# Weight sums queued behind the last turn, later x loads, spread gates and reordered splits in an S4 + SwiGLU kernel

## The chip, the cores and the metric

One core of one Trainium2 chip runs the whole kernel. The metric is the device time in microseconds of one execution; the number compared is the median over several runs. TensorE is called PE in the profile, VectorE DVE, ScalarE ACT, GpSimd POOL, and SyncE SP; SP does nothing here but issue DMAs.

## The reference

The input is a sequence of L = 2048 rows of D = 640 values. It passes through two residual branches, each with a layer norm whose scale, shift and gate come from a small product `silu(c) @ w_mod`:

```python
x = A_u
h = _layernorm(x) * (1 + ca) + sa
x = x + ga * _A_ref(h, ...)          # S4: a long convolution per channel, over the whole sequence
h = _layernorm(x) * (1 + cb) + sb
x = x + gb * _B_ref(h, w1, w3, w2)   # SwiGLU

def _B_ref(x, w1, w3, w2):           # w1, w3: 640 x 1728, w2: 1728 x 640
    return (silu(x @ w1) * (x @ w3)) @ w2
```

Everything is float32. The change touches the second branch alone.

## The kernel before

**Stages.** The first 420 us or so compute the convolution. Then the second branch runs on four column blocks of 512 sequence rows, taken in two pairs; in each pair the two blocks are called A and B. The hidden width of 1728 is cut into 14 tiles of 128, f = 0 to 13; the last tile is half full and holds the halves of w1 and w3 beside each other.

**Products in float32.** TensorE multiplies a rounded type. Each operand is therefore split into a high part (a cast on ACT) and a low part (operand minus high part, on DVE), and a product takes three matmuls: high by high, high by low, low by high. The weights' parts are `gh`, `gl` (from w1, loaded as `wg`) and `uh`, `ul` (from w3, loaded as `wu`); both come from tiles `rw` of which there are five. A "turn" (`turn_a`, `turn_b`) transposes one of the five 128-row slices k of the normalized x on TensorE, evacuates it with scale and shift on ACT into a raw tile `s`, and splits it into a pair of tiles: `xA…`, `xB…`, and for k = 0 and 1 of the B block `T3…`, printed as `T`.

**Plain tiles and blocks.** Pair 0 takes four tiles f = 0, 13, 1, 2 in the plain way (`plain`): a gate product of 15 matmuls of 128x512 and, but for f = 13, an up product of 15; first the A pass in that order, then the B pass in the reverse order, 2, 1, 13, 0. Its first input slices are turned while the A pass runs: k = 4, 0, 2 between the two products of the last A tile, k = 3 and 1 after it. The other ten tiles, and thirteen in pair 1, go through `seven`: one tile for both column blocks at once, by a scheme with seven products instead of eight, 54 matmuls in all. It is called a block below, numbered n = 0 to 9 in pair 0. It needs differences of the x slices (`x_sums`, four instructions for each i = 0, 1, two on DVE and two on POOL, then split into T1, T2, T4) and four weight sums S0 to S3 of the next block (`w_sums` on POOL, from `rw` to `S`; `w_split` makes `S0h`, `S0l` and so on, on ACT and DVE). S1 reads S0, and S3 reads S1.

**Gates of the output weights.** `gate_w2(f)` loads a tile of w2 into `rw`, multiplies it on POOL by the gate row `gbr`, and stores it in the scratch tensor `w2s` with a DMA that POOL issues. All 14 are done during the ten blocks of pair 0, in the order f = 0 to 13: one in each block, two in blocks n = 3 to 6. `outputs` later loads them again (`rw<-w2s`), in the order of the tiles in `order`.

**What sets the order.** A scheduler orders most instructions of the second branch on each engine; each engine and the DMA queue of SP then run in that order, and an instruction that waits holds all behind it. `with tc.issue_after(ins)` puts the instructions traced in it behind `ins` on the engine of `ins`. All of this stage's instructions are recorded by one helper, so they have one line, L102, in the profile; they are told apart by their tiles.

**The change of pairs.** While the outputs of pair 0 run, `prepare` lays out by a table of steps (`at(n, fn)`) the turns of pair 1, its x sums and splits, the weight loads of its first plain tile (f = 13) and first block, and their splits. The four x tiles that it starts with (`x_next`, from the six `xm` tiles) are loaded in the code of block n = 6, with `issue_after` on the last matmul of the block before; that binds TensorE's queue only, and the loads stand on SP.

Of the kernel before, what the change touches and what calls it, by code (L numbers as in the profile page):

```python
# [2 lines left out]

# [27 lines left out]
NFT = 14  # L31
# [76 lines left out]
def tile_kernel(ctx: ExitStack, tc: tile.TileContext, a):  # L108
# [917 lines left out]
    def x_sums(i, parts=range(4)):  # L1026

        b11, b21, b12, b22 = xraw["A", i], xraw["A", i + 2], xraw["B", i], xraw["B", i + 2]
        for p in parts:
            out, l, r = ((b11, b12, b11), (b12, b22, b12), (b22, b22, b11), (b21, b21, b22))[p]  # L1030
            (G if p % 2 else V).tensor_tensor(out, l, r, op=OP.subtract)
        xraw["T1", i], xraw["T2", i], xraw["T4", i] = b11, b22, b21

    def x_sum_split(i, names=("T1", "T2", "T4")):
        for n in names:
# [17 lines left out]
    def weight(f, name):  # L1053
        if (f, name) in ahead:
            return ahead.pop((f, name))
        w = xp.tile([P, KD, P], F32, name="rw", bufs=5)
        w = w.rearrange("p k c -> p (k c)") if name in ("w2", "gated") else w
        if name == "gated":
            SQ.dma_start(w, w2s[f])
            return w  # L1060
        with tc.issue_after(zlast[0].ins):
            w_get(w, f, name, SQ)
        return w

    def gate_w2(f):

# [27 lines left out]
        g = split(weight(f, "wg"), WS, ("gh", "gl"), after)  # L1094
        return g, split(weight(f, "wu"), WS, ("uh", "ul"), after) if f < NFT - 1 else None

    def plain(c, f, h, ws, early=False, between=None):

        last = f == NFT - 1
        wgs, wus = ws  # L1100
# [3 lines left out]
        if early and f == 0:  # L1104
            pu = bank(1)
            for lo in range(2):
                for k in range(KD):
                    for ps, ws in ((pg, wgs), (pu, wus)):
                        for i in range(1 if lo else 2):
                            end = PE.matmul(ps, ws[i][:, k, :], x[k][lo], start=(k + i + lo == 0),  # L1110
                                            stop=(lo == 1 and k == KD - 1))
        else:
            end = prod3(pg, [(wk(wgs, k), x[k]) for k in ks], True, True)
            if between:
                with tc.issue_after(end.ins):
                    between()
            if not last:
                pu = bank(1)
                end = prod3(pu, [(wk(wus, k), x[k]) for k in ks], True, True)
        sg = room(8)  # L1120
        if not last:
            S.activation(sg, pg, AF.Silu)
# [172 lines left out]
    def prepare(q0, g):  # L1295
# [30 lines left out]
            at(n, lambda i=i: x_mid(4 * q0 + i, got[i], g))  # L1326
        for n, i, p in ((21, 0, 0), (22, 0, 1), (23, 0, 2), (24, 0, 3), (24, 1, 0), (24, 1, 1), (25, 1, 2), (26, 1, 3)):
            at(n, lambda i=i, p=p: x_sums(i, (p,)))
        for n, i, name in ((22, 0, "T1"), (24, 0, "T2"), (26, 1, "T1"), (26, 1, "T2")):
            at(n, lambda i=i, name=name: x_sum_split(i, (name,)))  # L1330
        at(24, lambda: fetch(NFT - 1, "wg"))
        at(26, lambda: first_block.append(blocks(0)))
        at(27, lambda: first_plain.append(plain_weights(NFT - 1)))
        at(27, lambda: w_sums(first_block[0], range(4)))
        at(28, lambda: w_split(first_block[0], (1, 0, 2, 3)))

# [12 lines left out]
    last_f = NFT - 1  # L1349
    output = iter(())  # L1350
    x_next, first_block, first_plain = [], [], []
    ungated = list(range(NFT))
    for pair in range(2):
        q0 = 2 * pair
        hA, hB = {}, {}
# [1 line left out]
        rest = [f for f in range(last_f) if f not in simple]  # L1357
        side = []
        ws = first_plain.pop() if first_plain else plain_weights(simple[0], last_sum)
        if pair == 0:  # L1360
            tiles = []
            x_first(tiles)
# [10 lines left out]
            sp_order[0] = False  # L1373
            mid = lambda i: (x_mid(4 + i, got[i], 0), x_norm(4 + i, got[i], tiles))
            turn = lambda *ks: [turn_b(1, tiles, k, 0) for k in ks]
            side = [lambda: (mid(0), mid(1)), lambda: (mid(2), mid(3)), None, lambda: turn(3, 1)]
        for n, f in enumerate(simple):
            hA[f] = h_tile()
            ws = ws or plain_weights(f, ends if pair == 0 and n == 1 else None)
            end = plain("A", f, hA[f], ws, pair == 0, (lambda: turn(4, 0, 2)) if n == 3 else None)  # L1380
            if n < len(simple) - 1:
                ws = None
            todo = side.pop(0) if side else None
            if todo:
                with tc.issue_after(end.ins):
                    todo()
            if pair == 0 and n == 1:
                with tc.issue_after(power[0].ins):
                    for j, (x, z, st) in enumerate(early):
                        G.dma_start(xs[j], x)  # L1390
        turned = ends[1]

        for n, f in enumerate(simple[::-1]):
            hB[f] = h_tile()
# [11 lines left out]
        next(output, None)  # L1406
        free = []
        order = rest[:10] + ([0, last_f, 1, 2] if pair == 0 else [last_f] + rest[10:])
        output = outputs(q0, order, (hA, hB), prepare(q0 + 2, 1) if pair == 0 else lambda n: None, pair == 1)
        if first_block:  # L1410
            W = block_split(first_block.pop())
        else:
            W = blocks(rest[0])
            with tc.issue_after(turned.ins):
                block_split(W)
                w_sums(W, range(4))
                w_split(W, (1, 0, 2, 3))
        for n, f in enumerate(rest):
# [6 lines left out]
            hB[f] = h_tile()  # L1425
            if pair == 0 and n == len(rest) - 4:
                x_next += [x_tile() for _ in range(4)]
                with tc.issue_after(end.ins):
                    for i in range(4):
                        SQ.dma_start(x_next[i], a["x"][(8 + i) * P:(9 + i) * P, :])  # L1430
            gates = [gate_w2(g) for g in ungated[:1 + (3 <= n < 7)]] if pair == 0 else []
            ungated = ungated[len(gates):]
            if nxt is None:
                next(output)
# [55 lines left out]
```

## Time and profile before

| what | value |
|---|---|
| median of 3 runs | 1000.11 us (998.22 to 1000.22) |
| the profiled execution | 1002.07 us, of which 1000.3 us is the span from its first to its last instruction |
| PE busy in the span | 921.3 us |
| DVE, ACT, POOL busy | 698.9, 540.1, 293.9 us |
| mean granted TensorE clock | 0.947 of full speed |

The span is that of one execution under the hardware profiler. Where a row gives a time for an engine, it is the start counted from the first instruction, then the duration; what stands in square brackets is how long the engine was idle just before and what released it. "SPq" is SP issuing DMAs; its durations are the time that the queue took for them, waits included. In a row of the stretches, the share of an engine that is not the bound is no loss.

### The profile page before, as it was taken

How to read it: one execution, taken by the hardware profiler on the slowest of the kernel's cores; microseconds unless marked ns; L12 is line 12 of the kernel's file. 1: busy time of each engine (PE TensorE's matmuls, PEld its weight loads, DVE VectorE, ACT ScalarE, POOL GpSimd, SP SyncE). 2: the span in 40 equal slices, each digit the busy share in tenths (PEclk: the TensorE clock that was granted, in tenths of full speed). 3: DMA queues.
4: the chain of work that ended last, by engine and by line, in shares of the span. 5: the costliest groups of instructions: out<-in, count | busy, mean ns of one | idle time of the engine just before them, and what ended most of it. 6: DMA issues, size and time to landing. Idle time of an engine off the chain costs nothing.

```text
span 1000.3 us, 20632 instructions
## 1 busy us (share of the span) xinstructions
PE 921.3 (92%) x8214; PEld 688.3 (69%) x8214; DVE 698.9 (70%) x1227; ACT 540.1 (54%) x793; POOL 293.9 (29%) x302
## 2 busy tenths in 40 slices
PE   5898797998988888797999999999999999999997
PEld 2545354666666666465888778777878888888886
DVE  4598856888898885665678666667796666664544
ACT  3668665999999973245433323355743333323432
POOL 1453333544444531114444450111142222200000
PEclk9855777999999999999999999999999999999999
DMA  9463586554566687695334432897441111113443
GB/s 268 154 230 116 201 197 188 147 154 120 146 161 160 163 217 224 207 240 207 113 111 132 145 132 63 214 280 218 133 145 53 53 53 53 52 41 86 151 147 116
DMA packets 106659, 149.91 MB, mean 150 GB/s; under 512 B 20964, under 2 KB 63076, under 8 KB 106564
## 3 DMA queue, kind: packets, MB, share of 16 engines
q1 hardware_dynamic: 101636, 133.93, 45.8%
q0 software_dynamic: 3424, 12.33, 3.6%
q10 hardware_dynamic: 1504, 2.36, 0.8%
q8 instruction: 64, 1.05, 0.4%
q14 instruction: 31, 0.25, 0.1%
HBM read 112.53 MB, written 36.04 MB: 149 GB/s over the span
## 4 chain that ended last, share of the span: by engine, by line
PE 43%; DMA 5%; POOL 3%; DVE 2%; issue 1%; ACT 0%; DVEq 0%; SPq 0%; POOLq 0%
PE ps L102 43%; DMA rw<-in_w_dram 2%; DMA w2s<-rw 2%; POOL S L102 1%; POOL rw L102 1%; DMA xs<-xm 1%; DMA rw<-in_wu_dram 1%; DVE xm L102 1%; POOL s L102 0%; DVE T L102 0%; DVE gl L102 0%; DVE s L102 0%; DVE ul L102 0%; DVE h L102 0%; DVE S2l L102 0%
## 5 line engine op out<-in xcount | busy, mean ns | idle before, releaser
L102 DVE TENSOR_TENSOR s<-ps,s 128x512 f32<-128x512 f32 x138 | 94.6, 686 | 68.9 <-PE ps L102 68.0
L473 POOL TENSOR_TENSOR ph<-thi,iota 128x1024 int32<-128x1024 int32 x40 | 85.4, 2134 | 175.9 <-DVE A L509 78.2
L102 DVE TENSOR_TENSOR gl<-rw,gh 128x640 fp32r<-128x640 f32 x87 | 77.6, 892 | 78.0 <-ACT gh L102 77.0
L102 ACT CAST gh<-rw 128x640 fp32r<-128x640 f32 x87 | 63.3, 727 | 109.9 <-PE ps L102 95.9
L571 PE MATMUL p<-uk,s 128*64 128x256 f32 x640 | 79.1, 389 | 13.6 <-PE pa L433 5.6
L102 PE MATMUL ps<-xA,gh 128*128 128x512 f32 x280 | 87.7, 392 | 0.6 <-ACT xA L102 0.4
L102 PE MATMUL ps<-gh,uh 128*128 128x512 f32 x224 | 87.5, 391 | 0.0
L102 PE MATMUL ps<-gl,uh 128*128 128x512 f32 x224 | 87.2, 389 | 0.0
L102 PE MATMUL ps<-gh,ul 128*128 128x512 f32 x208 | 81.1, 390 | 0.0
L571 PEld LDWEIGHTS p<-uk,s 128*64 128x64 f32 x640 | 45.2, 138 | 38.9 <-PE pa L433 8.4
L102 POOL TENSOR_TENSOR S<-rw 128x256 f32<-128x256 f32 x46 | 36.6, 798 | 116.2 <-DVE S0l L102 87.2
L102 PEld LDWEIGHTS ps<-xA,gh 128*128 128x128 f32 x280 | 52.3, 188 | 13.6 <-ACT xA L102 1.0
L102 PE MATMUL ps<-xA,gl 128*128 128x512 f32 x140 | 54.6, 390 | 1.1 <-DVE gl L102 1.1
L136 ACT ACTIVATE A<-pa 128x1024 f32<-128x1024 f32 x40 | 40.4, 1023 | 25.8 <-PE pa L433 24.4
L498 DVE TENSOR_TENSOR E<-A,cs 128x1024 f32<-128x1024 f32 x40 | 51.0, 1275 | 1.7 <-ACT A L136 1.7
L505 DVE TENSOR_TENSOR A<-A,ph 128x1024 f32<-128x1024 f32 x40 | 50.1, 1253 | 0.0
L613 PE MATMUL pz<-Y,i 64*128 64x128 f32 x640 | 45.4, 286 | 5.1 <-issue 3.1
L613 PEld LDWEIGHTS pz<-Y,i 64*128 64x128 f32 x640 | 39.2, 191 | 14.9 <-issue 11.4
L102 PEld LDWEIGHTS ps<-gl,uh 128*128 128x128 f32 x224 | 42.1, 188 | 9.0
L102 PEld LDWEIGHTS ps<-gh,uh 128*128 128x128 f32 x224 | 42.0, 188 | 8.8
L540 PE MATMUL pt<-s,K 128*64 128x128 f32 x640 | 47.3, 291 | 0.5 <-ACT uk L139 0.5
L522 PE MATMUL pk<-E 128*32 128x64 f32 x1280 | 46.6, 232 | 1.2 <-DVE E L501 0.6
(257 smaller groups left out, 2333.5 us busy)
## 6 DMA issues: line engine op xcount, KB each, us to landing
rw<-w2s SPq DMA_DIRECT2D x56, 320.0 KB
us<-u SPq DMA_DIRECT2D x16, 640.0 KB
s<-in_s_dram SPq DMA_DIRECT2D x40, 256.0 KB
i<-in_i_dram SPq DMA_DIRECT2D x40, 256.0 KB
rw<-in_wg_dram SPq DMA_DIRECT2D x31, 320.0 KB
rw<-in_wu_dram SPq DMA_DIRECT2D x28, 320.0 KB
uk<-us SPq DMA_DIRECT2D x32, 256.0 KB
zs<-zt SPq DMA_DIRECT2D x32, 256.0 KB
```

The costliest lines, as they stand in the source:

```text
L102: ins = fn(*args, **kw)
L136: return tc.keep_in_program_order(S.activation(*args, **kw))
L473: hold(G.tensor_tensor(p, bc(thi[:, sl], 2, NPH), bc(iota, 1, SD), op=OP.mult))
L498: keep(V.tensor_tensor(EC[s][:, :, 1:3, :], AA[s][:, :, 1:3, :], mid(cs[s]), op=OP.mult))
L505: keep(V.tensor_tensor(A[:, :, 1:3, :], A[:, :, 1:3, :], mid(ph[s]), op=OP.mult))
L522: keep(PE.matmul(pk[dq * 32:dq * 32 + 32, g, :], x[:, g * 4 + dq, 1, :], x[:, g * 4 + dq, 0:3:2, :], start=(st == 0), stop=(st == 1), tile ...
L540: keep(PE.matmul(pt[c * 64:c * 64 + 64, g, :], kk[:, g, :], s1[:, c, :], start=True, stop=True, tile_position=(0, c * 64)))
L571: keep(PE.matmul(p2[par * 64:par * 64 + 64, pi, c, :], s2[:, pi * 2 + par, c * 64:c * 64 + 64], uk[:, 0:kn + 1:kn, f, :], start=True, stop ...
L613: ins = keep(PE.matmul(pz[:, par, (g % 2) * 2 + pi, :], i1[r, pi, c, :], Y[r, pi, c, :], start=(c == 0), stop=(c == 1), tile_position=(par ...
```

## The change

Five edits, all in the second branch:

1. The turns of k = 3 and 1 of the B block are issued behind the ninth matmul of the up product of the last A tile (`then`), instead of behind its end.
2. The first block's splits, sums and sum splits in pair 0 are queued behind the last turn's instructions on ACT and DVE (`turned` is now both of them) and behind the last x sum on POOL (`summed`), instead of behind DVE's alone.
3. The x tiles of pair 1 are loaded behind the weight loads of block n = 6 on SP (`loaded`).
4. The output weights are gated in the order in which they are used, one per block, two in blocks 3 and 6, three in block 9.
5. At the change of pairs, the split of T2 of i = 1 goes behind the weight split of the plain tile, and the first block's weight splits behind that.

```diff
@@ x_sums
-            (G if p % 2 else V).tensor_tensor(out, l, r, op=OP.subtract)
+            summed[0] = (G if p % 2 else V).tensor_tensor(out, l, r, op=OP.subtract)
+    @contextmanager
+    def behind(*instrs):
+        with ExitStack() as order:
+            for ins in instrs:
+                order.enter_context(tc.issue_after(ins.ins))
+            yield
@@ weight
-            w_get(w, f, name, SQ)
+            ins = w_get(w, f, name, SQ)
+        if name != "w2":
+            loaded[0] = ins
@@ plain
-                end = prod3(pu, [(wk(wus, k), x[k]) for k in ks], True, True)
+                terms = [(wk(wus, k), x[k]) for k in ks]
+                if then:
+                    end = prod3(pu, terms[:3], True, True)
+                    with tc.issue_after(end.ins):
+                        then()
+                    end = prod3(pu, terms[3:], False, True)
+                else:
+                    end = prod3(pu, terms, True, True)
@@ prepare
-        for n, i, name in ((22, 0, "T1"), (24, 0, "T2"), (26, 1, "T1"), (26, 1, "T2")):
+        for n, i, name in ((22, 0, "T1"), (24, 0, "T2"), (26, 1, "T1")):
...
         at(27, lambda: first_plain.append(plain_weights(NFT - 1)))
+        at(27, lambda: x_sum_split(1, ("T2",)))
         at(27, lambda: w_sums(first_block[0], range(4)))
@@ the pairs
-    ungated = list(range(NFT))
+    ungated = []
...
+        begin = list(ends)
...
-            side = [lambda: (mid(0), mid(1)), lambda: (mid(2), mid(3)), None, lambda: turn(3, 1)]
+            side = [lambda: (mid(0), mid(1)), lambda: (mid(2), mid(3))]
...
-            end = plain("A", f, hA[f], ws, pair == 0, (lambda: turn(4, 0, 2)) if n == 3 else None)
+            end = plain("A", f, hA[f], ws, pair == 0, *((lambda: turn(4, 0, 2), lambda: turn(3, 1)) if n == 3 else ()))
...
-        turned = ends[1]
+        turned = list(ends)
...
+        if pair == 0:
+            ungated = list(order)
...
-            W = block_split(first_block.pop())
+            with behind(*begin):
+                W = block_split(first_block.pop())
...
-            with tc.issue_after(turned.ins):
+            with behind(*turned, summed[0]):
...
-                with tc.issue_after(end.ins):
+                with tc.issue_after(loaded[0].ins):
                     for i in range(4):
                         SQ.dma_start(x_next[i], a["x"][(8 + i) * P:(9 + i) * P, :])
-            gates = [gate_w2(g) for g in ungated[:1 + (3 <= n < 7)]] if pair == 0 else []
+            gates = [gate_w2(g) for g in ungated[:3 if nxt is None else 1 + (n in (3, 6))]] if pair == 0 else []
```

POOL, at the start of the B pass of pair 0 (`s` are the raw slices in the x sums, `S` the weight sums from `rw`):

```order
+L102 TENSOR_TENSOR s_5710<-s_5720,s_5710 128x512
+L102 TENSOR_TENSOR s_5400<-s_5400,s_5720 128x512
+L102 TENSOR_TENSOR s_5749<-s_5740,s_5749 128x512
+L102 TENSOR_TENSOR s_5410<-s_5410,s_5740 128x512
 L102 TENSOR_TENSOR S_5964<-rw 128x256
 L102 TENSOR_TENSOR S_5972<-rw 128x256
 L102 TENSOR_TENSOR S_5968<-S_5964,rw 128x256
 L102 TENSOR_TENSOR S_5976<-rw,S_5968 128x256
-L102 TENSOR_TENSOR s_5710<-s_5720,s_5710 128x512
-L102 TENSOR_TENSOR s_5400<-s_5400,s_5720 128x512
-L102 TENSOR_TENSOR s_5758<-s_5749,s_5758 128x512
-L102 TENSOR_TENSOR s_5410<-s_5410,s_5749 128x512
```

The four x sums now stand ahead of the four weight sums of the first block.

ACT, at the same place, before and after (`s6`, `s7`, `s5` are the raw slices k = 2, 3, 1; `s8` is the silu of the last A tile; `T31` is the high part of k = 1):

```order
L102 CAST xB23_5722<-s6_5720 128x512
L102 CAST T120_5803<-s0_5381 128x512
L102 CAST S1h_5969<-S1_5968 128x256
L102 ACTIVATE s7_5749<-ps_5744,modT_66 128x512
L102 ACTIVATE s5_5758<-ps_5753,modT_66 128x512
L102 CAST xB23_5722<-s7_5749 128x512
```

```order
L102 CAST xB23_5722<-s6_5720 128x512
L102 ACTIVATE s7_5740<-ps_5735,modT_66 128x512
L102 ACTIVATE s5_5749<-ps_5744,modT_66 128x512
L102 CAST xB23_5722<-s7_5740 128x512
L102 CAST T31_5751<-s5_5749 128x512
```

The evacuations of k = 3 and 1 no longer stand behind the cast of a weight sum.

SP, before, at the weight loads of the last B tile (`rw_5905`) and of the first block (`rw_5952`, `rw_5954`), and after, at those of block 7 (`rw_6690`, `rw_6692`) and the two output weights gated in n = 6 (`rw<-in_w2`); `xm<-in_x` is an x tile of pair 1:

```order
L102 DMA rw_5905<-in_wu_dram 128x640
L102 DMA rw_5952<-in_wg_dram 128x640
L102 DMA xm_6714<-in_x_dram 128x640
L102 DMA xm_6715<-in_x_dram 128x640
L102 DMA rw_5954<-in_wu_dram 128x640
```

```order
L102 DMA rw_6690<-in_wg_dram 128x640
L102 DMA rw_6692<-in_wu_dram 128x640
L102 DMA xm_6704<-in_x_dram 128x640
L102 DMA xm_6705<-in_x_dram 128x640
L102 DMA xm_6706<-in_x_dram 128x640
L102 DMA xm_6707<-in_x_dram 128x640
L102 DMA rw_6712<-in_w2_dram 128x640
L102 DMA rw_6714<-in_w2_dram 128x640
```

Before, these four loads stood among the weight loads of the B pass, two of them just ahead of the last load of the first block. Now they stand between the loads of block 7 and the two gates of n = 6.

DVE, at the change of pairs (`gl` of `rw` 128x640 is the plain tile's weight split, `ul` 128x384 the first block's):

```order
 L102 TENSOR_TENSOR T_8205<-s_7664,T_8205 128x512
-L102 TENSOR_TENSOR T_8208<-s_8082,T_8208 128x512
 L102 TENSOR_TENSOR T_8328<-s_7768,T_8328 128x512
-L102 TENSOR_TENSOR ul<-rw,uh 128x384
-L102 TENSOR_TENSOR gl<-rw,gh 128x640
+L102 TENSOR_TENSOR gl<-rw,gh 128x640
+L102 TENSOR_TENSOR T_8231<-s_8082,T_8231 128x512
 L102 TENSOR_TENSOR xm<-ps,xm 128x512 x4
```

The plain tile's split now stands ahead of the T2 split; the block's split went further back, still ahead of the plain tile's `h`.

More of the change, by code (lines that the diff above doesn't have):

```diff
@@ L1 @@
 import math
-from contextlib import ExitStack
+from contextlib import ExitStack, contextmanager
 import numpy as np
@@ L1030, in x_sums @@
             out, l, r = ((b11, b12, b11), (b12, b22, b12), (b22, b22, b11), (b21, b21, b22))[p]
-            (G if p % 2 else V).tensor_tensor(out, l, r, op=OP.subtract)
+            summed[0] = (G if p % 2 else V).tensor_tensor(out, l, r, op=OP.subtract)
         xraw["T1", i], xraw["T2", i], xraw["T4", i] = b11, b22, b21
+    summed = [None]
+    @contextmanager
[4 more added lines that the diff above has]
+            yield
     def x_sum_split(i, names=("T1", "T2", "T4")):
@@ L1061, in weight @@
         with tc.issue_after(zlast[0].ins):
-            w_get(w, f, name, SQ)
+            ins = w_get(w, f, name, SQ)
+        if name != "w2":
+            loaded[0] = ins
         return w
+    loaded = [None]
     def gate_w2(f):
@@ L1095, in plain_weights, with plain @@
         return g, split(weight(f, "wu"), WS, ("uh", "ul"), after) if f < NFT - 1 else None
-    def plain(c, f, h, ws, early=False, between=None):
+    def plain(c, f, h, ws, early=False, between=None, then=None):
         last = f == NFT - 1
```

## The prediction

> **What bounds the kernel.** I read the page first (engines and clock), then TensorE's waits from the end of the convolution on, then the busy time of that part by stage, then the timelines of the queues at each wait.
>
> ```profile
> PE 921.3 (92%) x8214; PEld 688.3 (69%) x8214; DVE 698.9 (70%) x1227; ACT 540.1 (54%) x793; POOL 293.9 (29%) x302
> PEclk9855777999999999999999999999999999999999
> ```
>
> TensorE is busy 92% of the span and the busiest engine; its clock is full after the first fifth. So an edit to the second half is worth the TensorE waits that it removes, plus slow-clock time behind them. These are all its waits from 464 us to the end:
>
> ```profile
> PE ps L102 <- ACT xB L102: 4.5, 1, 4.5
> PE ps L102 <- DVE s L102: 3.0, 2, 1.9
> PE ps L102 <- DVE gl L102: 1.9, 2, 1.1
> PE ps L102 <- DVE xB L102: 1.7, 1, 1.7
> PE ps L102 <- DVE h L102: 0.2, 1, 0.2
> ```
>
> By stage (stretch, its length, then busy time of PE, PEld, DVE, ACT, POOL, the granted clock, DMA): the B pass of pair 0; blocks n=0 to 4; block 5; block 6; blocks 7 to 9; the change of pairs.
>
> ```profile
> 464.26:497.27 33.01, 26.79 (x109) 21.17 (x107) 18.95 (x26) 13.28 (x25) 14.27 (x15) 0.90 0.27 89
> 497.27:558.47 61.20, 61.20 (x272) 50.68 (x270) 46.94 (x70) 23.65 (x47) 29.18 (x32) 1.00 0.39 129
> 558.47:572.11 13.64, 12.55 (x55) 10.06 (x54) 8.28 (x14) 3.81 (x9) 6.96 (x8) 1.00 0.42 136
> 572.11:588.15 16.04, 14.18 (x55) 11.19 (x54) 9.15 (x16) 4.81 (x11) 5.67 (x7) 0.89 0.38 124
> 588.15:624.87 36.72, 36.72 (x163) 30.41 (x162) 24.32 (x37) 12.11 (x23) 10.41 (x12) 1.00 0.28 87
> 720.00:744.10 24.10, 21.95 (x95) 16.94 (x93) 24.00 (x31) 12.63 (x24) 12.34 (x11) 1.00 0.34 102
> ```
>
> The clean rows set the rate: 61.20 us for five blocks is 12.24 a block, and over 54 matmuls 0.2267 us each (36.72 for three blocks agrees). The B pass is 30+30+15+30 = 105 matmuls: 23.80 us clean, 33.01 measured, so 9.21 lost: 6.22 waiting (33.01 less 26.79 busy) and 2.99 at a lower clock (0.90). Block 5 loses 13.64 - 12.24 = 1.40, block 6 loses 16.04 - 12.24 = 3.80. These 14.4 us are what the change can reach there.
>
> **Part 1: weight sums queued behind the last turn, and the turn of k=3 and 1 put earlier.** The B pass as it is now, by engine (start, duration, instruction, idle time before it and its releaser):
>
> ```profile
> 464.26 0.72 PE L102 MATMUL ps<-xB,gh 128*128 128x512 f32 x2
> 471.12 0.79 PE L102 MATMUL ps<-xB,gh 128*128 128x512 f32 x1 [4.52 <-ACT xB L102]
> 474.47 0.80 PE L102 MATMUL ps<-xB,gh 128*128 128x512 f32 x1 [1.70 <-DVE xB L102]
> ...
> 458.28 2.23 SPq L102 DMA_DIRECT2D xm<-in_x_dram  x2
> ...
> 460.60 6.02 DMA rw<-in_wu_dram
> ...
> 466.70 1.40 POOL L102 TENSOR_TENSOR S<-rw 128x256 f32<-128x256 f32 x2 [8.92 <-DMA rw<-in_wu_dram]
> 469.54 1.26 POOL L102 TENSOR_TENSOR s<-s,s 128x512 f32<-128x512 f32 x1
> 471.61 1.66 POOL L102 TENSOR_TENSOR s<-s,s 128x512 f32<-128x512 f32 x1 [0.80 <-DVE s L102]
> ...
> 462.87 0.63 ACT L102 CAST xB<-s 128x512 fp32r<-128x512 f32 x1
> 468.81 0.41 ACT L102 CAST S1h<-S 128x256 fp32r<-128x256 f32 x1 [4.80 <-POOL S L102]
> 469.12 1.44 ACT L102 ACTIVATE s<-ps,modT 128x512 f32<-128x512 f32 x2
> 470.46 0.61 ACT L102 CAST xB<-s 128x512 fp32r<-128x512 f32 x1
> ...
> 462.04 0.69 DVE L102 TENSOR_TENSOR T<-s,T 128x512 fp32r<-128x512 f32 x1
> 470.84 0.69 DVE L102 TENSOR_TENSOR s<-s,s 128x512 f32<-128x512 f32 x1 [6.02 <-POOL s L102]
> 472.05 1.76 DVE L102 TENSOR_TENSOR s<-s,s 128x512 f32<-128x512 f32 x1
> ```
>
> The reader sees one knot. Two x loads hold SP's queue for 2.23 us, the weight load behind them lands 6.02 us after issue, and POOL sits 8.92 us on it with the x sums queued behind. ACT sits 4.80 us on POOL's S1 with the evacuation of k=3 queued behind; DVE sits 6.02 us on POOL's first x sum with the low half of k=3 queued behind. TensorE waits first for the high half (4.52), then for the low half (1.70).
>
> In the new order POOL has the x sums first, ACT goes from the cast of k=2 straight to the two evacuations, and the x loads are gone from SP here. TensorE does the transposes of k=3 and 1 after 9 of the 15 matmuls of the last A product, so they end 6 x 0.2267 = 1.4 us earlier; its work up to 464.26 is the same. Then from the rows: ACT is free at 462.87 + 0.63 = 463.50, begins the k=3 cast 470.46 - 469.12 = 1.34 later, and ends it 0.61 later, at 465.45. TensorE wants k=3 after 9 matmuls of the gate product, at 464.26 + 2.04 = 466.30, and its low half one matmul later, at 466.53. The high half is in time. The low half stands on DVE behind one x sum and the last A product's evacuation. POOL's first x sum can start when DVE has read its operand (462.04 + 0.69 = 462.73) and takes 1.26, to 464.0; then three DVE instructions of 0.69 (x sum, evacuation, low half) end at 466.1 to 466.3 if nothing stretches them. The row at 472.05 shows stretching: 1.76 instead of 0.69, beside a POOL sum that ran from 471.61 to 473.27, so DVE ended 0.54 after POOL. The second POOL x sum starts as DVE's x sum ends (about 464.9) and by 1.66 ends at 466.6; held until 0.54 after that, the low half comes at 467.1, 0.6 late. Bounds: no wait at all, or the rival below. I take 0.5, nearest to that one held instruction. Part 1: 9.2 - 0.5 = **8.7 us**.
>
> What was ahead is late next: ACT's and DVE's weight-sum splits now follow the x sums. Four x sums of 1.66 with a DVE step of 0.69 to 1.76 between each and the next take 9 to 12 us, to 472 or 475; four weight sums at 0.7 (the row at 466.70 holds two) end by 475 to 478. Their first user, the first block, starts at 464.26 + 23.8 = 488, so they are covered. The tighter user is the last B product, whose weight split stands behind the weight sums' casts on ACT (0.41 each, so by 480); it starts at 464.26 + 75 x 0.2267 = 481.3. Were that cover gone, it would wait; 0 to 1 us of this is in the range.
>
> **Part 2: the gates spread, and x loaded at block 6.** Waits at S3 (the product of the fourth weight sum) and what stood on POOL (rw<-rw,gbr is the gate of one output weight; the other rows end the S1 of blocks 6 and 7):
>
> ```profile
> 567.88 0.73 PE L102 MATMUL ps<-xB,S3h 128*128 128x512 f32 x2 [1.09 <-DVE s L102]
> 582.30 0.74 PE L102 MATMUL ps<-xB,S3h 128*128 128x512 f32 x2 [1.86 <-DVE s L102]
> ...
> 515.37 1.29 POOL L102 TENSOR_TENSOR rw<-rw,gbr 128x512 f32<-128x512 f32 x1 [3.93 <-DMA rw<-in_w_dram]
> 540.26 1.29 POOL L102 TENSOR_TENSOR rw<-rw,gbr 128x512 f32<-128x512 f32 x1 [1.26 <-DMA rw<-in_w_dram]
> 555.36 1.41 POOL L102 TENSOR_TENSOR rw<-rw,gbr 128x512 f32<-128x512 f32 x1 [2.57 <-DMA rw<-in_w_dram]
> 565.51 0.73 POOL L102 TENSOR_TENSOR S<-S,rw 128x256 f32<-128x256 f32 x1
> 569.56 1.47 POOL L102 TENSOR_TENSOR rw<-rw,gbr 128x512 f32<-128x512 f32 x1 [1.75 <-DMA rw<-in_w_dram]
> 579.95 0.73 POOL L102 TENSOR_TENSOR S<-S,rw 128x256 f32<-128x256 f32 x1
> ...
> 544.38 2.87 DMA rw<-in_w_dram
> ```
>
> Two gates per block take 15.10 us (540.26 to 555.36) and 14.20 (to 569.56), since a gate's load waits for the store of the one before; a block takes 12.24. So the weight sums behind them fall later each block. S1 ends at 566.24 and 580.68, and TensorE goes on 1.64 and 1.62 later; S3 is due 36 matmuls (8.16 us) into a block, so S1 is due 6.5 into it: at 565.0 and 578.6. It came 1.2 and 2.0 late, which are the two waits.
>
> Now blocks 4 and 5 have one gate, about 7.3 us, instead of two, against 12.24. Two stay at n=3, where no wait is seen, two at n=6, three at n=9. Block 6 in the frame of the old times: the first of two gates at n=3 ran at 515.37, 6.4 before block 2 started (497.27 + 2 x 12.24 = 521.75); so the first at n=6 would run at 558.47 - 6.4 = 552.1. The four x loads now stand just ahead of its load: two of them made a load take 6.02 instead of 2.87, so four cost about 6.3: 558.4. Two more gate periods of 7.3 (the last belongs to n=7 and stands ahead of S1) and the sums give S1 of block 7 at 558.4 + 14.6 + 1.3 + 0.7 = 575.0, due at 558.47 + 12.24 + 6.5 = 577.2. Covered by 2 us. At n=9 three gates stand ahead of the last block's sums; begun after the gate of n=8, itself one period per block early, they need 3 x 7.3 = 22 us at worst for two blocks of 24.5. I take both waits and the slow clock gone: 1.40 + 3.80 = **5.2 us** (bounds 0 and 5.2).
>
> The 3.80 rests on the clock. The wait of block 6 was only 1.86; the other 1.94 goes with a granted clock of 0.89. The Trainium skill ("TensorE: Matmul & The Clock Gate", Part 1, What's actually happening) has the clock halved only after an idle window of about 3.4 us. By it block 6 would give back 1.86, not 3.80, and the sum would be 1.9 smaller. The stage's row differs, and decides.
>
> **Part 3: splits at the change of pairs.**
>
> ```profile
> 734.52 0.50 PE L102 MATMUL ps<-xA,gl 128*128 128x512 f32 x1 [1.12 <-DVE gl L102]
> 744.15 0.73 PE L102 MATMUL ps<-xA,gh 128*128 128x512 f32 x2 [0.22 <-DVE h L102]
> ...
> 743.40 0.69 DVE L102 TENSOR_TENSOR h<-ps,s 64x512 f32<-64x512 f32 x1
> ```
>
> The gl split now precedes a T split and a weight split, so the wait of 1.12 goes. But DVE is busy 24.00 of 24.10 us up to h, and the same instructions stand ahead of h as before, only in another order. So h ends at 744.09 again, and TensorE, 1.12 earlier at it, waits 0.22 + 1.12 there. I take **0** (bounds 0 and 1.3).
>
> **Sum.** 8.7 + 5.2 + 0 = 13.9 us. The profiled execution had 1002.07 (1.8 around its span of 1000.3), 0.2% above the median 1000.11; it gives 988.2, the median 986.2.
>
> **The rivals.**
> - POOL beside DVE. The x sums now fall beside the last turn's splits. If one more DVE instruction is held, the low half of k=3 comes at 467.8, 1.3 late, and that of k=1 (T) up to 1.9; with slow clock as behind the wait of 1.86, part 1 loses 1.4 + 1.9 = 3.3 more: 989.5. For: the row at 472.05. Against: the evacuation of h between them reads only one SBUF tensor. The Trainium skill ("GPSIMD Engine Reference", Specifications) names this: both engines share their SBUF interfaces, with contention for DVE instructions with two SBUF inputs; that row agrees.
> - The gates' delay moves instead of going: the x loads or the three gates bring S1 of block 7 or 9 late, cover 2 us, and part 2 gives nothing: 991.4.
> - DVE follows: the sums on POOL fall elsewhere, h comes 1.3 earlier: 984.9.
> - Slower: the x loads are served one after another ahead of block 6's gate. Four times 6.02 puts the load from 549.2 to 573.3 + 2.9 = 576.2 and S1 of block 6 near 580, 15 late against 565.0; with 1.9 of clock that is 16.9, and 1003. It decides from an arrival at about 573 on. Against: the two at 458.28 cost 1.6 each.
>
> **Chances.** Forecast 0.60 (own range 984.9 to 987.6), first rival 0.16, second 0.13, third 0.06, slower 0.03, and 0.02 that it all stays within 0.2%, which is about what a measurement of this kernel can tell from no change. So faster 0.95. The range takes the third rival with a microsecond of run-to-run spread (the runs span 2.0) and the second: 983.9 to 991.5.
>
> **What the profile after would show.** Part 1: no TensorE wait over 1 us between 464 and 490, ACT's S1h no longer ahead of the evacuations, the B pass 24 to 25 us. Part 2: block starts 12.24 apart through all ten blocks, no wait for DVE s. Part 3: the wait for gl gone and one of about 1.3 for h. The prediction is wrong if the low half of k=3 is over 1 us late, or if S1 ends more than 6.5 us into a block.

## The result, and the profile after

The changed kernel took 994.59 us (median of 8 runs, 990.54 to 997.91), the kernel before, in turn with it, 999.88 (8 runs, 996.78 to 1003.90): ratio 0.9946, 95% interval 0.9921 to 0.9971. It is faster, by less than forecast: 994.59 lies 8.4 us above the 986.2 predicted and outside its range. A second comparison gave 993.77 against 1003.19, ratio 0.9905 [0.9885, 0.9924]. The changed kernel's two medians lie 0.8 us apart; those of the kernel before moved by 3.3.

The profiled execution after took 993.24 us, 8.83 less than the 1002.07 of before. From here on the kernels are compared by stage, since the work ahead of the B pass, which the change leaves alone, ended anywhere from 459.41 to 466.78 us in the fourteen profiles of this study.

| profile | B pass begins | B pass | blocks 0 to 9 | first output product to last matmul | B pass begin to last matmul |
|---|---|---|---|---|---|
| before | 464.26 | 33.01 | 127.60 | 370.00 | 530.61 |
| after | 464.06 | 24.76 | 126.62 | 369.99 | 521.37 |
| gain | 0.20 | **8.25** | **0.98** | **0.01** | 9.24 |
| forecast | 0 | 8.7 | 5.2 | 0 | 13.9 |

So parts 1 and 3 did as forecast, and part 2 gave 0.98 of 5.2. On the page, TensorE is busy 93% of the span instead of 92%, with 917.3 us of work instead of 921.3.

All waits of TensorE from 464 us to the end (sum, count, longest):

```profile
PE ps L102 <- DVE s L102: 3.3, 3, 1.6
PE ps L102 <- DVE h L102: 1.7, 1, 1.7
PE ps L102 <- DVE gl L102: 0.8, 1, 0.8
PE ps L102 <- DVE xB L102: 0.7, 1, 0.7
```

The wait for ACT (4.5) is gone, that for DVE's xB fell from 1.7 to 0.7, one of two for gl went. The waits for DVE s, which part 2 was to remove, are three instead of two and sum to 3.3 instead of 3.0. So the 0.98 does not come from shorter waits: in this profile of before, block 6 also lost 1.94 us to a slow clock, and no block after does.

By stage, columns as before (length; PE, PEld, DVE, ACT, POOL; granted clock, DMA): B pass; blocks 0 to 4; blocks 5, 6 and 8; the change of pairs.

```profile
464.06:488.82 24.76, 24.09 (x106) 19.63 (x105) 19.07 (x27) 12.81 (x25) 14.94 (x13) 1.00 0.22 67
488.82:550.02 61.20, 61.20 (x271) 50.69 (x270) 43.29 (x70) 23.78 (x47) 23.93 (x28) 1.00 0.43 139
550.02:563.11 13.09, 12.54 (x56) 10.06 (x54) 8.62 (x14) 3.82 (x8) 6.58 (x9) 1.00 0.43 155
563.11:577.24 14.13, 12.53 (x55) 10.06 (x54) 10.78 (x16) 5.02 (x11) 4.62 (x6) 1.00 0.42 139
...
589.48:603.20 13.72, 12.54 (x55) 10.06 (x54) 11.79 (x16) 5.12 (x11) 7.61 (x9) 1.00 0.59 192
710.60:734.66 24.06, 21.61 (x95) 17.01 (x93) 23.97 (x31) 12.46 (x24) 12.46 (x11) 1.00 0.32 92
```

The B pass runs at full clock. Blocks 0 to 4 are clean (12.24 each), blocks 5, 6 and 8 are 0.85, 1.89 and 1.48 us longer. Before, only 5 and 6 were. TensorE's own rows show where:

```profile
467.17 0.50 PE L102 MATMUL ps<-xB,gh 128*128 128x512 f32 x1 [0.68 <-DVE xB L102]
558.89 0.73 PE L102 MATMUL ps<-xB,S3h 128*128 128x512 f32 x2 [0.55 <-DVE s L102]
573.03 0.73 PE L102 MATMUL ps<-xB,S3h 128*128 128x512 f32 x2 [1.60 <-DVE s L102]
596.94 0.73 PE L102 MATMUL ps<-xB,uh 128*128 128x512 f32 x2 [1.18 <-DVE s L102]
734.73 0.73 PE L102 MATMUL ps<-xA,gh 128*128 128x512 f32 x2 [1.66 <-DVE h L102]
```

### The profile page after: what moved, and what is told of

Read it like the earlier page. It is cut to its first block, busy times and chain, and to the rows that moved or that the text cites. A ratio compares the mean times of both kernels' runs of the same rounds, so it can differ in the third digit from the quotient of the medians.

```text
span 990.8 us, 20630 instructions
## 1 busy us (share of the span) xinstructions
PE 917.3 (93%) x8214; PEld 686.5 (69%) x8214; DVE 700.4 (71%) x1227; ACT 539.7 (54%) x793; POOL 292.7 (30%) x302
## 3 DMA queue, kind: packets, MB, share of 16 engines
q8 instruction: 64, 1.05, 0.5%
## 4 chain that ended last, share of the span: by engine, by line
PE 66%; ACT 15%; DVE 10%; DMA 3%; issue 3%; POOL 3%; DVEq 0%; ACTq 0%; SPq 0%; POOLq 0%
PE ps L102 49%; ACT cs L136 4%; PE p L571 3%; ACT A L136 3%; ACT ph L136 3%; PE pa L433 2%; ACT L136 2%; PE pq L445 2%; PE pz L613 2%; PE pt L540 1%; PE pk L522 1%; PE pm L300 1%; DMA rw<-in_w_dram 1%; PE pu L407 1%; DVE A L505 1%
```

## The experiments

The theory on part 2: the gates' delay has only moved, because the blocks now start earlier than the gates can follow, and the x loads and the three gates at the end add to it. Its rivals: the x loads alone do it; any block with two gates does it, wherever it stands; it is scatter between executions. Every kernel below starts from the changed one unless it says otherwise. All profiles in one table, in us; "rest" is the time from the first output product to the last matmul, and the waits are those of TensorE in the blocks:

| kernel | B pass | blocks | rest | waits in the blocks (block) | time, ratio to before [95%] |
|---|---|---|---|---|---|
| before_again | 34.03 | 126.31 | 370.0 | 1.53 (5), 1.79 (6) | one run, 1001.09 |
| after_again | 24.81 | 126.25 | 370.0 | 0.76 (5), 1.51 (6), 0.67 (8) | 993.77, 0.9905 [0.9885, 0.9924] |
| turn_only | 24.82 | 130.70 | 370.0 | 0.97, 2.22, 2.04, 0.25 (3 to 6) | 998.82, 0.9963 [0.9947, 0.9978] |
| x_early | 24.76 | 124.60 | 370.0 | 0.39 (6), 1.14 (8) | 993.12, 0.9889 [0.9865, 0.9913] |
| even_xearly | 24.82 | 128.26 | 370.0 | 1.31 (3), 1.92 (5), 1.29 (7) | 997.23, 0.9943 [0.9919, 0.9968] |
| even | 24.78 | 130.45 | 370.0 | 1.42 (3), 0.21 (5), 2.63 (6) | 998.36, 0.9971 [0.9957, 0.9986] |
| splits_back | 24.83 | 128.68 | 370.0 | 1.33 (5), 1.82 (6), 0.60 (8) | 994.44, 0.9917 [0.9888, 0.9945] |
| front4_xearly | 24.83 | 129.61 | 370.0 | 0.66, 0.28 (3), 1.56, 1.90 (4) | one run, 995.55 |
| sums_first | 24.82 | 125.47 | 370.0 | 0.65 (5), 1.76 (6) | 991.49, 0.9915 [0.9882, 0.9948] |
| sums_first_xearly | 24.82 | 124.32 | 370.0 | 1.61 (3) | 992.11, 0.9920 [0.9893, 0.9947] |
| tail5 | 24.79 | 122.40 | 370.0 | none | 987.66, 0.9875 [0.9841, 0.9909] |
| tail4 | 24.80 | 123.55 | 370.0 | 0.85 (3) | one run, 988.86 |

The kernel before had a median of 1003.19 beside the first four, 1002.62 beside the next four, 1001.44 beside the last four. The intervals overlap for most pairs of kernels, so the conclusions rest on the stages. The B pass (24.76 to 24.83 in all twelve profiles with edits 1 and 2) and the rest repeat well. The blocks do less: 126.62 and 126.25 for the changed kernel, 127.60 and 126.31 for the one before, and each other kernel was profiled once.

### before_again and after_again: both kernels unchanged

> The kernel before, unchanged, profiled once more, to see what varies between executions of one program. If only the first stage (up to the B pass of pair 0) varies, the B pass takes 33.0 us again, blocks 0 to 9 take 127.6 and the rest to the last matmul 370.0, each within 0.3, and the span differs only by where the B pass starts. If the waits themselves vary, the B pass or the blocks differ by 1 to 4 us.

> The changed kernel, unchanged, profiled once more and timed. The two profiles so far differ by 9.4 us, the medians by 5.3. If the profiles are right and the medians carry the first stage's scatter, the ratio here is about 0.991 and the B pass takes 24.8 us, the blocks 126.6. If the waits in the blocks vary between executions, the blocks take 125 to 130 and the ratio stays near 0.995.

From the B pass on the second pair of profiles differs by 9.27 us (530.34 against 521.07), the first by 9.24. The stage gains do not repeat one by one: the B pass gave 9.22 this time, the blocks 0.06. So the waits themselves vary between executions of the kernel before, and part 2's gain of 0.98 is not one that repeats. Blocks 5 and 6 of before_again:

```profile
558.65:572.72 14.07, 12.54 (x56) 10.06 (x54) 8.37 (x15) 3.79 (x10) 6.79 (x8) 1.00 0.44 135
572.72:587.04 14.32, 12.53 (x55) 10.06 (x54) 8.83 (x16) 4.83 (x11) 4.90 (x6) 1.00 0.42 138
```

Block 6 waits 1.79 here and lasts 14.32; in the first profile it waited 1.86 and lasted 16.04. So the 1.94 us of slow clock that the prediction counted in the 3.80 is not there in every execution. With 1.83 and 2.08 over in blocks 5 and 6, what the change could reach there was 3.9 us in this one, against 5.2.

### turn_only: the earlier turn alone (edits 1 and 2)

```diff
-            gates = [gate_w2(g) for g in ungated[:3 if nxt is None else 1 + (n in (3, 6))]] if pair == 0 else []
+            gates = [gate_w2(g) for g in ungated[:1 + (3 <= n < 7)]] if pair == 0 else []
-                with tc.issue_after(loaded[0].ins):
+                with tc.issue_after(end.ins):
```

With it the gates' old order (`ungated = list(range(NFT))`) and edit 5 undone, so edits 3, 4 and 5 are out.

> Only the edits on the turn and on the queueing of the first sums; x loads, gates and the splits at the change of pairs as before. Theory: the B pass gives 8.2 us (24.8 instead of 33.0) whatever the gates do, and the blocks keep their two waits of 1.1 and 1.9 and 127.6 us in all: ratio 0.992. Rival: with the two x loads back ahead of the first block's last weight load, POOL's weight sums come late again and part of the gain goes: B pass over 26 us. Second rival: blocks start earlier against the same chain of gates and loads, so the waits grow: blocks 129 us or more.

The B pass, and all ten blocks:

```profile
464.56:489.38 24.82, 24.15 (x107) 19.64 (x106) 19.87 (x27) 12.82 (x25) 15.01 (x13) 1.00 0.22 66
489.38:620.08 130.70, 125.22 (x541) 102.20 (x540) 85.36 (x135) 43.79 (x87) 51.38 (x58) 0.99 0.38 123
```

Part 1 gives its 8.2 alone. But the blocks, with exactly the gates and x loads of before, last 130.70 instead of 127.60 and wait in four blocks, the first already in block 3: 3.1 us of part 1 are given back (one block has about 1.9 us of slow clock in both profiles; against before_again, which has none, it is 4.4). POOL's gates show why, the very first before, then the very first and the first of n=3 in turn_only:

```profile
489.04 1.29 POOL L102 TENSOR_TENSOR rw<-rw,gbr 128x512 f32<-128x512 f32 x1
```

```profile
486.59 1.29 POOL L102 TENSOR_TENSOR rw<-rw,gbr 128x512 f32<-128x512 f32 x1 [1.49 <-issue]
513.29 1.30 POOL L102 TENSOR_TENSOR rw<-rw,gbr 128x512 f32<-128x512 f32 x1 [5.12 <-DMA rw<-in_w_dram]
```

Before, the gate at 515.37 ran 6.4 ahead of the start of block 2. Here it runs at 513.29, block 2 starts at 513.86: 0.6 ahead. The blocks came 7.9 earlier (489.38 against 497.27), the first gate 2.45 and this one 2.1. From the first gate to this one it is 26.3 us before and 26.7 here: the gates have a pace of their own, and the B pass's waits had given them their lead.

So measured from turn_only the other edits did bring something: 130.70 less 126.62 is 4.1 us. Of it, 3.1 went into paying for the earlier start.

### x_early: the x loads back at their old place

```diff
-                with tc.issue_after(loaded[0].ins):
+                with tc.issue_after(end.ins):
```

> The change with the x loads put back where they were; gates in their new places. Theory (the four x loads ahead of block 6's gates delay them and with them S1 of blocks 6 and 7): the waits of 0.55 and 1.60 in blocks 5 and 6 go, that of 1.18 in block 8 (three gates ahead of the last sums) stays, the blocks take 124 us instead of 126.6, ratio 0.3% below the changed kernel's. Rival (the two gates of block 6 alone, each waiting for the store of the one before, are too slow): the waits stay over 1.5 us in sum and the blocks take 126 or more.

Block 6, and POOL's first gate of n=6:

```profile
565.02:577.94 12.92, 12.53 (x55) 10.06 (x54) 7.91 (x15) 4.37 (x10) 4.92 (x6) 1.00 0.44 130
...
551.41 1.29 POOL L102 TENSOR_TENSOR rw<-rw,gbr 128x512 f32<-128x512 f32 x1 [5.12 <-DMA rw<-in_w_dram]
```

The B pass does not get longer (24.76): once the sums are queued behind the turn, the x loads on SP there cost it nothing. The ten blocks last 124.60, 2.0 us less than after (1.65 less than after_again). Block 5 is clean and block 6 waits 0.39 instead of 1.60. So edit 3 costs about 2 us in the blocks, and edit 4 is worth about 6.1 (130.70 less 124.60) once the blocks start early, of which 1.9 is the slow clock of one block in turn_only. The x loads alone are not the cause: two waits are left.

### even_xearly, even, front4_xearly: other places for the four extra gates

```diff
-            gates = [gate_w2(g) for g in ungated[:3 if nxt is None else 1 + (n in (3, 6))]] if pair == 0 else []
+            gates = [gate_w2(g) for g in ungated[:1 + (n in (1, 3, 5, 7))]] if pair == 0 else []
```

This is `even`; `even_xearly` has the edit of x_early too; `front4_xearly` has that and `1 + (n < 4)`.

> The change with the x loads where they were and the four extra gates in blocks 1, 3, 5 and 7 (two there, one in all others, none bunched at the end). Theory (a chain of gates: one gate takes 7.2 us from multiply to multiply since its load waits for the store before; two in one block take 14.4 against 12.24, but two blocks with three gates take 21.6 against 24.5, so an even spread has no wait): blocks 0 to 9 take 122.4 to 123.2 us, no wait for S3 or in block 8, ratio to before 0.986 to 0.988. Rival (any block with two gates is late now that blocks start 8 us earlier and the chain has lost its lead): waits of 0.5 to 1 us in blocks 2, 4 and 6, blocks 124 us or more.

> The same even spread, but the x loads behind the weight loads of block 6 as in the change. If the x loads are what delays the gates of block 6 by about 5 us, a wait of 0.5 to 2 us shows in block 5, 6 or 7 and the blocks take 123 to 125. If only the bunches of gates did, the blocks take under 123 like the kernel beside it.

> The change with x loads early and two gates in each of blocks 0 to 3, one after. Chain theory: four blocks with two gates take 4 x 14.4 = 58 us against 49, so S1 falls later by 2.2 us a block and waits of 1 to 2 us show in two or three of blocks 1 to 4, and none after; blocks 125 to 128. Rival (only the late blocks lack a lead, the early ones have one): no wait, blocks under 123.

Block 5 of even_xearly:

```profile
551.86:566.31 14.45, 12.53 (x56) 10.06 (x54) 8.28 (x15) 4.37 (x10) 4.89 (x6) 1.00 0.51 169
```

Blocks 3, 5 and 7 have two gates each there, and wait 1.31, 1.92 and 1.29. That three gates in two blocks fit, because 3 x 7.2 is under 2 x 12.24, fell: from the first gate of n=3 (513.14) to the first of n=5 (539.59) it took 26.45 us, 7.2 between the two of n=3 and 9.7 and 9.6 from one block's last gate to the next block's first. The rival's length, 124 us or more, came, but not its waits of 0.5 to 1 us in blocks 2, 4 and 6.

With the x loads at block 6, `even` lasts 2.2 us more, but this is not the price of the loads: its waits sum to 4.26 against 4.52, and 3.15 us of its length are slow clock in block 6 (18.02 long, wait 2.63, clock 0.81). What differs is the place of the waits: blocks 5 and 7, with two gates each, are nearly or wholly clean, and block 6, with one, waits most. In front4_xearly the waits came in blocks its theory named: 3 and 4 pay (13.77 and 17.91 us), the five after them are clean. The sum of its waits, 4.40, is no better, and the blocks take 129.61, over the 128 of the theory. So the place of the extra gates changes the place of the loss more than its size, as long as all four stand in blocks 0 to 7.

Why two gates in one block cost more than two periods is argued only: each gate also takes one of the buffers `rw` that the next weights need, and SP's queue waits for them. In block 9 of the changed kernel, which has no next weights to load, three gates run 2.2 us apart. No run had one more buffer.

### splits_back: edit 5 undone

```diff
-        for n, i, name in ((22, 0, "T1"), (24, 0, "T2"), (26, 1, "T1")):
+        for n, i, name in ((22, 0, "T1"), (24, 0, "T2"), (26, 1, "T1"), (26, 1, "T2")):
-        at(27, lambda: x_sum_split(1, ("T2",)))
-            with behind(*begin):
-                W = block_split(first_block.pop())
+            W = block_split(first_block.pop())
```

> The change with the reordering at the change of pairs undone. Theory (DVE is busy throughout up to h, so the order ahead of h is worth nothing): the wait of 1.12 for gl comes back, that of 1.66 for h falls to about 0.2, and from the first output product to the last matmul it is 370.0 us again, within 0.2; ratio within 0.2% of the changed kernel's. Rival (the edit is worth its wait): 1.1 us longer.

TensorE's last two waits at the change of pairs:

```profile
727.51 0.50 PE L102 MATMUL ps<-xA,gl 128*128 128x512 f32 x1 [1.09 <-DVE gl L102]
737.15 0.73 PE L102 MATMUL ps<-xA,gh 128*128 128x512 f32 x2 [0.23 <-DVE h L102]
```

The wait for gl is back (1.09), that for h is 0.23 instead of 1.66, and from the first output product (617.87) to the last matmul (987.84) it is 369.97 against 369.99. Edit 5 is worth nothing. The blocks of this run last 2.1 more than after, but edit 5 acts behind them: 1.6 of that is slow clock in block 6 (15.98 long with a wait of 1.82).

### sums_first, sums_first_xearly: the last three gates behind the sums of block 9

```diff
-            G.tensor_tensor(t[0], l, r, op=OP.subtract if n else OP.add)
+            added[0] = G.tensor_tensor(t[0], l, r, op=OP.subtract if n else OP.add)
...
-        for g in gates:
-            g()
+        with ExitStack() as order:
+            if not nxt and gates:
+                order.enter_context(tc.issue_after(added[0].ins))
+            for g in gates:
+                g()
```

> The changed kernel, with the three gates of block 9 queued on POOL behind the weight sums of block 9 instead of ahead of them; nothing else. Theory (these gates hold S1 of block 9): the wait in block 8 (1.18 and 0.67 us in two profiles, 1.0 to 1.5 us of length) goes and block 8 takes 12.24; the waits in blocks 5 and 6 stay; blocks 125.2 us, ratio to before 0.1% below the changed kernel's. Rival (block 8 waits for weight loads that come late, whatever the order on POOL): the wait stays.

> The same with the x loads where they were. Theory: of the waits in the blocks only that of block 6 is left (two gates, 0.4 us), blocks 122.8 to 123.3 us, ratio 0.987 to 0.988. Rival: as in the even spread, waits over 1 us come up elsewhere and the blocks take over 125.

Block 8 of sums_first:

```profile
585.22:597.46 12.24, 12.24 (x56) 10.13 (x54) 9.71 (x15) 4.70 (x10) 5.83 (x6) 1.00 0.67 208
```

Block 8 goes from 13.72 to 12.24, and the waits of blocks 5 and 6 stay. So the place of the three gates on POOL costs the 1.48 us of block 8. But late sums are not the way it does, though the theory had it so. S1 of block 9 ended at 595.74 in the changed kernel, 6.26 us into block 8. What TensorE waited for there is the sum that DVE makes of a product at 596.21, with DVE's split of S1 queued behind it, at 596.81. POOL's last two gates and S1, then DVE, after:

```profile
589.56 1.32 POOL L102 TENSOR_TENSOR rw<-rw,gbr 128x512 f32<-128x512 f32 x1
591.77 1.29 POOL L102 TENSOR_TENSOR rw<-rw,gbr 128x512 f32<-128x512 f32 x1
594.80 0.94 POOL L102 TENSOR_TENSOR S<-S,rw 128x256 f32<-128x256 f32 x1
...
589.47 2.10 DVE L102 TENSOR_TENSOR gl<-rw,gh 128x640 fp32r<-128x640 f32 x1
591.49 2.14 DVE L102 TENSOR_TENSOR h<-s,s 128x512 f32<-128x512 f32 x1
596.21 0.68 DVE L102 TENSOR_TENSOR s<-ps,s 128x512 f32<-128x512 f32 x1
```

Beside the gates, DVE's instructions took 2.10 and 2.14 us where the same two took 0.82 and 0.69 in block 7; the next two beside POOL's sums, `ul` and `A`, took 0.99 and 1.22 instead of 0.55 and 0.68. Together that is 3.7 us more. after_again and x_early have the same durations within 0.02. In sums_first the gates run beside DVE as well, but the same four take only 1.8 us more (1.05, 1.78, 1.05 and 0.68), and no wait shows. That it is this difference which removes the wait is read from the rows; no run changed it alone.

With the x loads early as well, blocks 6 and 8 are both clean, and one wait of 1.61 shows in block 3, which has two gates; the blocks take 124.32, between the two forecasts. x_early is the same program up to there and had no wait. The first gate of n=3 ran at 514.10 in sums_first_xearly, 0.2 ahead of block 2, and at 514.46 in x_early, 1.6 ahead. So what that gate's lead is varies from one execution to another, and the wait with it. In time the two kernels sums_first and sums_first_xearly can't be told apart (0.9915, 0.9920).

### tail5, tail4: no block with two gates, and one

Both have the edits of x_early and sums_first, and

```diff
+            gates = [gate_w2(g) for g in ungated[:5 if nxt is None else 1]] if pair == 0 else []
```

in tail5; tail4 has `4 if nxt is None else 1 + (n == 3)`.

> x loads where they were, one gate in each of blocks 0 to 8, five in block 9 behind its sums. Theory (the lead of the gates over the blocks is lost only where a block has two gates): no wait in blocks 0 to 8, 122.4 us for all ten, ratio 0.986 to 0.987, unless the five gates delay the reloads of the output weights: then a wait of up to 3 us shows in the first output products. Rival (one gate per block is too much too, now that the blocks start 8 us earlier): waits of 0.3 to 1 us in blocks 3 to 8.

> As the one before, with two gates in block 3 and four in block 9. Theory: like it, but S1 of block 4 comes about 2 us later in its block than that of block 3 or 5, with no wait or one under 0.3 us in blocks 3 to 5. If one extra gate anywhere costs a wait, one of 1 to 2 us shows in block 3, as in the even spread.

The ten blocks of tail5:

```profile
487.09:609.49 122.40, 122.40 (x541) 101.35 (x540) 85.48 (x135) 45.41 (x87) 51.74 (x58) 1.00 0.40 129
```

Ten blocks of 12.24, TensorE busy in all 122.40 us, no wait for DVE s. The five gates behind block 9's sums (from 584.31 on) are done before their users: the rest is 370.0 again. tail4 differs in one gate, moved from block 9 to block 3, and has one wait, 0.85 in block 3 (13.40 long); under 0.3 was expected there, or 1 to 2 if one extra gate costs as in the even spread, and it came between. Its first gate of n=3 (511.32) ran 0.9 ahead of block 2 (512.20). With that of turn_only (0.6, wait 0.97) and of sums_first_xearly (0.2, wait 1.61), and no wait in the five profiles with a lead of 1.6 to 2.0 (after, after_again, splits_back, sums_first, x_early), the wait in block 3 follows the lead.

tail5 has the lowest ratio, 0.9875 [0.9841, 0.9909]. 987.66 is 3.8 below sums_first of the same comparison, though the two intervals overlap, and its blocks are 4.2 us shorter than those after. They are 5.2 shorter than before: the prediction's gain for part 2 could be had, in this one profile, by another order than the change's.

## Why the prediction was right or wrong

**Part 1: right, 8.25 against 8.7** (9.22 in the second pair of profiles). The chain ran as worked out. The cast of k=3 on ACT, the low halves of k=2 and k=3 on DVE, and POOL's second x sum, after:

```profile
464.39 0.64 ACT L102 CAST xB<-s 128x512 fp32r<-128x512 f32 x1
...
463.20 1.19 DVE L102 TENSOR_TENSOR xB<-s,xB 128x512 fp32r<-128x512 f32 x1 [0.81 <-ACT xB L102]
465.71 1.41 DVE L102 TENSOR_TENSOR xB<-s,xB 128x512 fp32r<-128x512 f32 x1
...
465.27 1.30 POOL L102 TENSOR_TENSOR s<-s,s 128x512 f32<-128x512 f32 x1 [1.42 <-DVE s L102]
```

The high half of k=3 was due to end at 465.45 and ended at 465.03, the low half at 467.1 and ended at 467.12: held beside POOL's second x sum for 1.41 us, it ended 0.55 after POOL's, where 0.54 was assumed. TensorE waited 0.68 (0.5 forecast). A second DVE instruction was held too (463.20, 1.19 us), which is the first rival's condition, but it lay earlier and cost no wait of 1.4 and no clock. The weight sums and splits behind the turn stayed covered. The B pass lasts 0.96 more than the clean 23.80, of which 0.68 is this wait.

**Part 3: right, 0.01.** The wait of 1.12 went and the one for h became 1.66 (1.34 forecast), with DVE busy 23.97 of the 24.06 us ahead of it; splits_back shows the same sum without the edit.

**Part 2: wrong, 0.98 against 5.2.** The step that failed is "the first of two gates at n=3 ran at 515.37, 6.4 before block 2 started (521.75); so the first at n=6 would run at 558.47 - 6.4 = 552.1". It was worked in the frame of the old times, as if the gates kept their place against the blocks when part 1 moved the blocks. They didn't. The first gate's load, DVE's split of the last plain tile's weight ahead of it, and three gates, before and after:

```profile
485.25 0.33 SPq L102 DMA_DIRECT2D rw<-in_w_dram  x1
...
484.40 0.82 DVE L102 TENSOR_TENSOR gl<-rw,gh 128x640 fp32r<-128x640 f32 x1 [0.18 <-ACT gh L102]
```

```profile
480.99 0.33 SPq L102 DMA_DIRECT2D rw<-in_w_dram  x1
545.20 1.84 SPq L102 DMA_DIRECT2D xm<-in_x_dram  x4
547.14 10.96 SPq L102 DMA_DIRECT2D rw<-in_w_dram  x2
...
480.14 0.82 DVE L102 TENSOR_TENSOR gl<-rw,gh 128x640 fp32r<-128x640 f32 x1
...
485.09 1.29 POOL L102 TENSOR_TENSOR rw<-rw,gbr 128x512 f32<-128x512 f32 x1 [0.49 <-DVE h L102]
511.58 1.30 POOL L102 TENSOR_TENSOR rw<-rw,gbr 128x512 f32<-128x512 f32 x1 [5.04 <-DVE S3l L102]
553.29 1.29 POOL L102 TENSOR_TENSOR rw<-rw,gbr 128x512 f32<-128x512 f32 x1 [9.59 <-DMA rw<-in_w_dram]
...
547.14 6.00 DMA rw<-in_w_dram
```

Block 0 starts 8.45 us earlier (488.82), the first gate only 3.95 (485.09 against 489.04): its load goes out right behind that split, which came 4.26 earlier and no more, and the gate follows the issue of the load by 3.8 and 4.1. By n=3 the lead over block 2 (513.30) is 1.7 instead of 6.4. turn_only gives the price of the earlier start by itself, 3.1 us.

That the lead at n=6 would be that of n=3 held: without the x loads in the way (x_early) the first gate of n=6 ran at 551.41, 1.3 ahead of block 5 (552.74), where 6.4 was counted on. After, it ran at 553.29, 3.3 behind the start of block 5 (550.02), where "558.4" in the old frame put it level. So the four x loads made it 4.6 later, where 6.3 was assumed: the load behind them was issued at 547.14 and took 6.00. That term was too large; the lead is what was missing.

The other half of the step's margin was that S1 need only end 6.5 us into a block. S1 of block 6 ended at 556.57 (the row at 555.82 below), 6.55 into block 5, and that of block 7 at 570.11 (the row at 569.37), 7.0 into block 6: 0.05 and 0.5 late, yet TensorE waited 0.55 and 1.60. What made up the difference stands on DVE, with POOL's sums beside it (before, in block 6, then after, in blocks 5 and 6):

```profile
581.15 0.49 DVE L102 TENSOR_TENSOR S1l<-S,S1h 128x256 fp32r<-128x256 f32 x1 [5.36 <-ACT S1h L102]
581.32 0.91 POOL L102 TENSOR_TENSOR S<-rw,S 128x256 f32<-128x256 f32 x1
```

```profile
557.05 1.19 DVE L102 TENSOR_TENSOR S1l<-S,S1h 128x256 fp32r<-128x256 f32 x1 [3.34 <-ACT S1h L102]
570.58 1.79 DVE L102 TENSOR_TENSOR S1l<-S,S1h 128x256 fp32r<-128x256 f32 x1 [3.23 <-ACT S1h L102]
...
555.82 0.75 POOL L102 TENSOR_TENSOR S<-S,rw 128x256 f32<-128x256 f32 x1
...
557.21 0.74 POOL L102 TENSOR_TENSOR S<-rw,S 128x256 f32<-128x256 f32 x1
...
569.37 0.74 POOL L102 TENSOR_TENSOR S<-S,rw 128x256 f32<-128x256 f32 x1
570.65 0.76 POOL L102 TENSOR_TENSOR S<-rw 128x256 f32<-128x256 f32 x1
571.35 0.73 POOL L102 TENSOR_TENSOR S<-rw,S 128x256 f32<-128x256 f32 x1
```

The low split of S1 took 0.49 before. After, it took 1.19 and 1.79, each time until 0.29 after POOL's last sum. Less the 0.70 and 1.30 of that, the two waits would be none and 0.3. So the first rival's mechanism, DVE held beside POOL, came in a place where the prediction had not looked for it, and makes most of the waits in blocks 5 and 6. Part 2 of the prediction put it at nothing, without a reason; this is the second step that failed. The same two durations (1.19 to 1.20 and 1.79 to 1.80) stand in blocks 5 and 6 of after_again and splits_back and of sums_first, all with the x loads at block 6 and the extra gates at n=3, 6 and 9; in x_early it is 0.41 and 0.51. What brings it is open. Late sums alone do not: in turn_only and in block 6 of even S1 came late and its split took 0.49 to 0.50. No run moved the split alone.

"At n=9 three gates stand ahead of the last block's sums ... they need 3 x 7.3 = 22 us at worst for two blocks of 24.5" missed block 8, which lost 1.48; sums_first takes it away. The term itself was on the safe side: the three gates ran 2.2 us apart, and S1 behind them came 6.26 into block 8, in time. What was left out is again POOL beside DVE, 3.7 us on four of DVE's instructions (the rows under sums_first).

Finally 1.94 of the 5.2 was a single execution's slow clock; the second profile of before has 0.3 there. Part 2's term was at most about 3.9 in that one.

The second rival ("the gates' delay moves instead of going … part 2 gives nothing", 991.4) came near in size. Of its conditions one held, S1 of block 7 late behind the x loads, by 0.5 us; that of block 9 did not. The two causes that weigh more it did not name: the blocks' earlier start, and DVE held beside POOL. The sum against the profiled execution: 1002.07, less 8.25, 0.98 and 0.01 for the parts and 0.26 at the two ends of the program, plus 0.67 (2.44 around the span instead of 1.77), is 993.24.

## What to carry to other kernels

When one edit makes a stage start earlier, work out every later queue again in the new times: a chain that fed on the removed wait keeps its own pace, and its slack is spent first. Of a side job that shares an engine's queue with work on the critical path, put one piece in each turn even if the total time per turn would hold more, and ask which other engine's instructions it will run beside. Price a wait that came with a slow clock by the wait alone until a second profile shows the rest again.

## What the runs showed of the hardware

A wait of about 2 us sometimes costs as much again in clock, and sometimes not. What a block with one wait lasts beyond 12.24 and its wait: 1.94 (before, wait 1.86), 1.92 (splits_back, 1.82), 3.15 (even, 2.63), but 0.29 (before_again, 1.79), 0.30 (sums_first, 1.76), 0.29 (even_xearly, 1.92), and within turn_only, in two blocks in a row:

```profile
539.61:554.37 14.76, 12.54 (x56) 10.06 (x54) 8.23 (x15) 3.80 (x9) 6.97 (x9) 1.00 0.41 132
554.37:570.55 16.18, 14.14 (x55) 11.19 (x54) 9.91 (x16) 4.81 (x11) 6.86 (x8) 0.89 0.43 144
```

After a wait of 2.22 the first loses 0.30 at full clock; after 2.04 the second loses 1.90 at 0.89. In the blocks with one wait of up to 1.61 whose length was taken, none lost more than 0.34. By the idle window of about 3.4 us in the Trainium skill ("TensorE: Matmul & The Clock Gate", Part 1, What's actually happening) none of these waits should have cost any clock. Here four of the eight from 1.76 to 2.63 did, and what decides it is not shown.

DVE's instructions were held beside POOL's: some with two inputs in SBUF that took 0.41 to 0.82 us in other blocks took 0.99 to 2.14 (the rows of blocks 5, 6 and 8 after). Which of the two engines gives way is not always the same. Where S1's split on DVE and a POOL sum began within 0.2 us of each other, POOL's sum took 0.91 instead of 0.74 and DVE's split 0.49 before; after, POOL's took 0.74 and DVE's 1.19. In both, POOL's sum before that one was still running when the split began (580.64 to 581.36, and 556.52 to 557.26). The recorded starts lie 0.17 and 0.16 apart, so what decides it is not to be read from them and stays open.
